# Attention with 192 queries and 1024 keys: transposed scores, an exponential straight from PSUM without a row maximum, and row sums from a ones column beside V

## The chip, the cores and the metric

The kernel runs on one core of one Trainium2 chip. Times are device microseconds (us) of that core, medians of several runs. The runs that are compared here are of the fast state (the records know a slower one, with longer times at a lower granted clock); one of the four runs of b4_gpsimd was slow and is left out. Each batch of runs had the kernel before run beside it on the same chip (1265.0 to 1265.2 us every time). Trace times are counted from the start of the profiled span.

## The reference

```python
B, H, Sq, Sk, D = 16, 32, 192, 1024, 128          # bf16; q, k, v are normal * 0.05
def reference(q, k, v):
    scale = q.shape[-1] ** -0.5
    scores = jnp.einsum("bhqd,bhkd->bhqk", q, k) * scale
    p = _softmax(scores, axis=-1)
    return jnp.einsum("bhqk,bhkd->bhqd", p, v)
```

There are 512 heads. K and V hold 134 MB each, Q and the output 25 MB each: 319 MB have to pass the DMA engines whatever the kernel computes.

## The kernel before

Heads go in groups of 16, two groups of buffers. A pair of heads makes three units of 128 query rows (128 of each head, then 64 of both side by side). Per unit: QK into PSUM with queries on the partitions, a row maximum on VectorE, a shift on GpSimd or an exponential on ScalarE, eight transposes on TensorE, an evacuation through ScalarE (with the exponential where the shift was on GpSimd), then PV. All loads and stores are issued by SyncE, on one queue:

```python
                e.dma_start_transpose(
                    kt[:, s], kf[h0:h0 + G].rearrange("g k d -> (g k) d")
                ).then_inc(sxk[s], 16)
                e.dma_start_transpose(
                    qt[:, s], qf[h0:h0 + G].rearrange("g k d -> (g k) d")
                ).then_inc(sxq[s], 16)
                if g >= NS:
                    e.wait_ge(s_pv, last_u + 1)
                e.dma_start(
                    vs[:, s], vf[h0:h0 + G].rearrange("g (p t) d -> p g t d", t=KT_TILES)
                ).then_inc(svl[s], 16)
```

```python
            def tr(u):                       # TensorE: the transposes that the change removes
                # ... waits ...
                for t in range(KT_TILES):
                    ins = pe.transpose(PT[:, t, :], X[:, t: SK: KT_TILES], ident[:])
                ins.then_inc(s_tr, 1)
            # ...
                dve.tensor_scalar(           # VectorE: row maximum (as a minimum of the negated scores)
                    ss[:, u % NSS, :], s_ps[u % 2][:], -scale, None, ALU.mult, ALU.min,
                    accum_out=nb[:, u % NSS: u % NSS + 1],
                ).then_inc(s_max, 1)
```

V's key order is `8 p + t`, so that each partition reads 2 KB that lie together, and one transfer brings the V of 16 heads.

## Time and profile before

| | before |
|---|---|
| time, median | 1265 us |
| TensorE busy | 1234 us (98%) |
| VectorE, ScalarE, GpSimd busy | 1102, 1049, 960 us |
| a group of 16 heads, from its first QK to the next group's | 38.4 us |

In the profile PE is TensorE and PEld its weight loads, DVE is VectorE, ACT ScalarE, POOL GpSimd, and SPq the queue of SyncE. The profile's page gives busy time and share of the span (part 1), the busy tenths of DMA in 40 slices (part 2), the queues (part 3: packets, MB, share), and the chain that ended last (part 4):

```profile
PE 1234.2 (98%) x20480; PEld 1009.4 (80%) x20480; DVE 1102.0 (87%) x2304; ACT 1048.6 (83%) x1281; POOL 960.4 (76%) x518
...
DMA  9999999999999999999999999999999999999941
...
DMA packets 790743, 321.89 MB, mean 255 GB/s; under 512 B 724992, under 2 KB 724992, under 8 KB 790528
...
q1 hardware_dynamic: 790528, 318.78, 108.8%
q8 instruction: 164, 2.69, 0.8%
...
PE 97%; SPq 1%; DMA 1%; ACT 0%; issue 0%; DVE 0%; ACTq 0%
```

TensorE bounds the kernel: it is busy all the time and is nearly all of the chain. But the line of DMA tenths says 9 in every slice but the last two. The queue's own timeline, columns: start, duration, engine, line, operation, tiles, count.

```profile
177.74 16.89 SPq L141 DMA_TRANSPOSE kt<-in_k_dram  x1
194.67 4.06 SPq L144 DMA_TRANSPOSE qt<-in_q_dram  x1
198.77 0.59 SPq L149 DMA_DIRECT2D vs<-in_v_dram  x1
199.41 4.60 SPq L158 DMA_DIRECT2D out_dram<-ob  x1
204.05 9.72 SPq L163 DMA_DIRECT2D out_dram<-ob  x1
213.82 0.63 SPq L164 DMA_DIRECT2D out_dram<-ob  x1
214.49 18.25 SPq L141 DMA_TRANSPOSE kt<-in_k_dram  x1
...
595.90 19.96 SPq L141 DMA_TRANSPOSE kt<-in_k_dram  x1
...
637.11 17.95 SPq L141 DMA_TRANSPOSE kt<-in_k_dram  x1
```

Here the queue had fallen behind and waited for no compute: what its loads and its first store wait for had been met at least 4.6 us earlier. This cycle of 16 heads takes 36.8 us (177.74 to 214.49).

### The profile page before, as it was taken

How to read it: one execution, taken by the hardware profiler on the slowest of the kernel's cores; microseconds unless marked ns; L12 is line 12 of the kernel's file. 1: busy time of each engine (PE TensorE's matmuls, PEld its weight loads, DVE VectorE, ACT ScalarE, POOL GpSimd, SP SyncE). 2: the span in 40 equal slices, each digit the busy share in tenths (PEclk: the TensorE clock that was granted, in tenths of full speed). 3: DMA queues.
4: the chain of work that ended last, by engine and by line, in shares of the span. 5: the costliest groups of instructions: out<-in, count | busy, mean ns of one | idle time of the engine just before them, and what ended most of it. 6: DMA issues, size and time to landing. Idle time of an engine off the chain costs nothing.

```text
span 1263.1 us, 48658 instructions
## 1 busy us (share of the span) xinstructions
PE 1234.2 (98%) x20480; PEld 1009.4 (80%) x20480; DVE 1102.0 (87%) x2304; ACT 1048.6 (83%) x1281; POOL 960.4 (76%) x518
## 2 busy tenths in 40 slices
PE   3999999999999999999999999999999999999997
PEld 1888888888888888888888888888888888888886
DVE  2889888898988989898898988889898898989885
ACT  1888888888888888888888888888888888888886
POOL 2778777777877778787777877777787777878774
PEclk9999999999999999999999999999999999999999
DMA  9999999999999999999999999999999999999941
GB/s 288 268 261 240 278 280 266 288 270 245 254 269 261 279 233 255 281 275 262 261 230 272 271 276 268 252 251 272 272 267 281 253 263 252 271 261 281 244 118 27
DMA packets 790743, 321.89 MB, mean 255 GB/s; under 512 B 724992, under 2 KB 724992, under 8 KB 790528
## 3 DMA queue, kind: packets, MB, share of 16 engines
q1 hardware_dynamic: 790528, 318.78, 108.8%
q8 instruction: 164, 2.69, 0.8%
q14 instruction: 51, 0.42, 0.1%
HBM read 134.22 MB, written 25.17 MB: 126 GB/s over the span
## 4 chain that ended last, share of the span: by engine, by line
PE 97%; SPq 1%; DMA 1%; ACT 0%; issue 0%; DVE 0%; ACTq 0%
PE pt_ps L244 33%; PE o_ps L267 24%; PE s_ps L215 18%; PE o_ps L273 11%; PE s_ps L222 9%; SPq L141 1%; DMA vs<-in_v_dram 1%; PE o_ps L270 1%; PE o_ps L275 1%; SPq L144 0%; PE s_ps L228 0%; ACT x_sb L356 0%; ACT pt_sb L367 0%; DVE ob L330 0%; DVE rinv L327 0%
## 5 line engine op out<-in xcount | busy, mean ns | idle before, releaser
L188 POOL TENSOR_TENSOR x_sb<-ss,nb 128x1024 bf16<-128x1024 f32 x512 | 959.7, 1895 | 288.9 <-PE pt_ps L244 266.8
L300 DVE TENSOR_SCALAR_CACHE_REDUCE ss<-s_ps 128x1024 f32<-128x1024 f32 x768 | 938.5, 1222 | 140.5 <-PE s_ps L215 110.8
L244 PEld LDWEIGHTS pt_ps<-ident,x_sb 128*128 128x128 bf16 x6144 | 487.1, 148 | 203.3 <-issue 105.4
L367 ACT ACTIVATE pt_sb<-pt_ps 128x1024 bf16<-128x1024 bf16 x512 | 521.0, 1018 | 41.9 <-PE pt_ps L244 41.8
L244 PE MATMUL pt_ps<-ident,x_sb 128*128 128x128 bf16 x6144 | 520.7, 228 | 0.2 <-ACT pt_sb L367 0.2
L267 PE MATMUL o_ps<-vs,pt_sb 128*128 128x128 bf16 x4096 | 403.0, 217 | 0.3 <-DMA vs<-in_v_dram 0.3
L369 ACT ACTIVATE pt_sb<-pt_ps 128x1024 bf16<-128x1024 bf16 x256 | 262.1, 1024 | 140.1 <-PE pt_ps L244 140.0
L270 PE MATMUL o_ps<-ones,pt_sb 128*128 128x1 bf16 x4096 | 376.0, 165 | 0.0
L267 PEld LDWEIGHTS o_ps<-vs,pt_sb 128*128 128x128 bf16 x4096 | 352.3, 97 | 0.5 <-DMA vs<-in_v_dram 0.4
L270 PEld LDWEIGHTS o_ps<-ones,pt_sb 128*128 128x128 bf16 x4096 | 340.7, 96 | 0.0
L215 PE MATMUL s_ps<-kt,qt 128*128 128x512 bf16 x1024 | 305.3, 379 | 21.3 <-DMA qt<-in_q_dram 21.0
L356 ACT ACTIVATE x_sb<-ss,nb 128x1024 bf16<-128x1024 f32 x256 | 292.3, 1142 | 23.6 <-DVE ss L300 23.6
L273 PE MATMUL o_ps<-vs,pt_sb 128*64 128x128 bf16 x2048 | 162.3, 222 | 0.0
L275 PE MATMUL o_ps<-vs,pt_sb 128*64 128x128 bf16 x2048 | 162.3, 222 | 0.0
L222 PE MATMUL s_ps<-kt,qt 128*64 128x512 bf16 x512 | 153.2, 381 | 0.6 <-DVE ss L300 0.5
L228 PE MATMUL s_ps<-kt,qt 128*64 128x512 bf16 x512 | 153.2, 381 | 0.0
L330 DVE TENSOR_TENSOR ob<-o_ps,rinv 128x384 bf16<-128x384 f32 x256 | 142.7, 557 | 8.7
L273 PEld LDWEIGHTS o_ps<-vs,pt_sb 128*64 128x64 bf16 x2048 | 121.0, 109 | 17.1
L275 PEld LDWEIGHTS o_ps<-vs,pt_sb 128*64 128x64 bf16 x2048 | 121.0, 109 | 0.0
L215 PEld LDWEIGHTS s_ps<-kt,qt 128*128 128x128 bf16 x1024 | 63.3, 96 | 23.6 <-issue 21.5
L300 DVE DVE_READ_ACCUMULATOR ss<-s_ps 128x1 f32 x768 | 64.0, 83 | 0.0
L356 ACT ACTIVATION_READ_ACCUMULATOR x_sb<-ss,nb 128x1 f32 x256 | 48.9, 191 | 0.0
(11 smaller groups left out, 165.7 us busy)
## 6 DMA issues: line engine op xcount, KB each, us to landing
vs<-in_v_dram SPq DMA_DIRECT2D x32, 4096.0 KB, 15.2
out_dram<-ob SPq DMA_DIRECT2D x32, 512.0 KB, 15.9
out_dram<-ob SPq DMA_DIRECT2D x64, 128.0 KB, 4.9
kt<-in_k_dram SPq DMA_TRANSPOSE x32, 21.4
qt<-in_q_dram SPq DMA_TRANSPOSE x32, 6.6
```

Source lines behind the costliest of these rows:

```text
L188: gp.tensor_tensor(x_sb[:, u % NX, :], ss[:, u % NSS, :], nb[:, u % NSS: u % NSS + 1].to_broadcast([128, SK]), ALU.subtract,).then_inc(s_x ...
L215: ins = pe.matmul(S[:, cs], qt[:, s, x * SQ: x * SQ + 128], kt[:, s, x * SK + 512 * c: x * SK + 512 * c + 512], start=True, stop=True,)
L222: pe.matmul(S[0:64, cs], qt[:, s, a * SQ + 128: a * SQ + 192], kt[:, s, a * SK + 512 * c: a * SK + 512 * c + 512], start=True, stop=True, ...
L244: ins = pe.transpose(PT[:, t, :], X[:, t: SK: KT_TILES], ident[:])
L267: ins = pe.matmul(O[:, sl, :], PTS[:, t, :], vs[:, s, x, t, :], start=first, stop=last, skip_group_check=True)
L270: ins = pe.matmul(O[:, 3, sl: sl + 1], PTS[:, t, :], ones[:, 0:1], start=False, stop=last, skip_group_check=True)
L273: pe.matmul(O[0:64, sl, :], PTS[:, t, 0:64], vs[:, s, a, t, :], start=first, stop=last, skip_group_check=True, tile_position=(0, 0))
L275: ins = pe.matmul(O[64:128, sl, :], PTS[:, t, 64:128], vs[:, s, b, t, :], start=first, stop=last, skip_group_check=True, tile_position=(0, ...
L300: dve.tensor_scalar(ss[:, u % NSS, :], s_ps[u % 2][:], -scale, None, ALU.mult, ALU.min, accum_out=nb[:, u % NSS: u % NSS + 1],).then_inc(s ...
L356: act.activation(x_sb[:, u % NX, :], ss[:, u % NSS, :], ACT_FN.Exp, bias=nb[:, u % NSS: u % NSS + 1], scale=-1.0, accum_out=rs[:, pr % NRS ...
L367: act.activation(pt_sb[:, u % NPT], pt_ps[u % 2][:], ACT_FN.Exp, scale=-1.0).then_inc(s_eva, 1)
L369: act.activation(pt_sb[:, u % NPT], pt_ps[u % 2][:], ACT_FN.Copy).then_inc(s_eva, 1)
```

## The change

The intent is to take transposes, row maximum, shift and evacuation away. QK is computed transposed (keys on the partitions), so that its exponential is at once the stationary operand of PV. The maximum is left out; the row sums come from a ones column that stands beside V in SBUF; at the end the sums are checked for range, and where one falls outside, the whole of the kernel before runs as a general path. The diff, cut to its core:

```diff
+def _attention_kernel(nc, q, k, v, out, GM=8, NS=4):        # groups of 8 heads, four buffers
+    NSO = 3
+    VB = 288
+            vs = sb("f_vs", [128, NS, GM * 4 + 1, VB], BF16)
+                    if g >= NS:
+                        e.wait_ge(s_qk, first[g - NS] + sizes[g - NS])
+                    e.dma_start_transpose(
+                        kt[:, s, 0:T * n * 128].rearrange("d (t m) -> d t m", t=T),
+                        kf[h0:h0 + n].rearrange("g (m t) d -> (g m) (t d)", t=T),
+                    ).then_inc(s_kq[s], 16)
+                    ... # Q likewise, then a wait for the buffer's last PV
+                    for i in range(n):
+                        e.dma_start(
+                            vs[:, s, 4 * i: 4 * i + 4, 32:VB],
+                            vf[h0 + i].rearrange("(p u t) d -> p u (t d)", u=4, t=2),
+                        ).then_inc(s_v[s], 16)
+    ... # TensorE: QK transposed
+                                ins = pe.matmul(
+                                    S[:, c0: c0 + (j1 - j0) * 64],
+                                    kt[:, s, w0: w0 + 128], mv, start=True, stop=True)
+    ... # TensorE: PV, the ones column left of even tiles and right of odd ones
+                            c0 = b * VB + (31 if t % 2 == 0 else 160)
+                            ins = pe.matmul(
+                                O[64 * x: 64 * x + 64, o0: o0 + 129],
+                                pt[:, (h + x) % NP, t * SQ + j * 64: t * SQ + j * 64 + 64],
+                                vrow[:, c0: c0 + 129], ...)
+    ... # ScalarE: one instruction per head
+                    act.activation(pt[:, h % NP, :], s_ps[h % 2][:], ACT_FN.Exp, scale=scale).then_inc(s_exp, 1)
```

To put a ones column beside every tile, two tiles (512 bytes) are followed by a gap of 64 bytes in SBUF. V no longer travels in runs of 2 KB but in runs of 512 bytes, and by one transfer a head.

More of the change, by code (lines that the diff above doesn't have):

```diff
@@ L13, with _only_if, wrap, run @@
 R_W = 2
-def _attention_kernel(nc, q, k, v, out, G=16, NS=2, LAGS=(2, 4, 5, 7), ROUTES=(R_W, R_W, R_EA)):
+def _only_if(redo):
+    def wrap(body):
+        def run(eng):
+            with eng.register() as r:
+                eng.reg_load(r, redo[0:1, 0:1])
+                with eng.If_ne(r, 0):
+                    body(eng)
+        return run
+    return wrap
+def _general_path(nc, q, k, v, out, redo, G=16, NS=2, LAGS=(2, 4, 5, 7), ROUTES=(R_W, R_W, R_EA)):
     B, H, SQ, D = q.shape
@@ L133, in _ @@
         @block.sync
+        @_only_if(redo)
         def _(e):
@@ L176, in _ @@
         @block.gpsimd
+        @_only_if(redo)
         def _(gp):
@@ L197, in _ @@
         @block.tensor
+        @_only_if(redo)
         def _(pe):
@@ L294, in _ @@
         @block.vector
+        @_only_if(redo)
         def _(dve):
@@ L347, in _ @@
         @block.scalar
+        @_only_if(redo)
         def _(act):
@@ L377, in _, with _group_sizes, sem, sb @@
                     exp_first(u)
+QK_TILED = False
+RS_LO = 2.0 ** -40
+RS_HI = 2.0 ** 20
+def _group_sizes(NH):
+    if NH >= 32:
+        return [2, 2, 4] + [8] * ((NH - 16) // 8) + [4, 2, 2]
+    return [2] * (NH // 2)
+def _attention_kernel(nc, q, k, v, out, GM=8, NS=4):
+    B, H, SQ, D = q.shape
+    SK = k.shape[2]
+    assert D == 128 and SK == 1024 and SQ == 192, (D, SK, SQ)
+    NH = B * H
+    NPR = NH // 2
+    T = SK // 128
+    scale = float(D) ** -0.5
+    sizes = _group_sizes(NH)
+    assert sum(sizes) == NH
+    first = [sum(sizes[:i]) for i in range(len(sizes))]
+    NG = len(sizes)
+    gof = [g for g in range(NG) for _ in range(sizes[g])]
+    NP = 6
+    NSO = 3
+    VB = 288
+    qf = q.rearrange("b h s d -> (b h) s d")
+    kf = k.rearrange("b h s d -> (b h) s d")
+    vf = v.rearrange("b h s d -> (b h) s d")
+    of = out.rearrange("b h s d -> (b h) s d")
+    with ExitStack() as outer:
+        redo = outer.enter_context(nc.sbuf_tensor("redo", [1, 1], mybir.dt.int32))
+        def sem(name):
+            return outer.enter_context(nc.semaphore(name))
+        s_set = sem("f_set")
+        s_kq = [sem("f_kq%d" % i) for i in range(NS)]
+        s_v = [sem("f_v%d" % i) for i in range(NS)]
+        s_st = [sem("f_st%d" % i) for i in range(NSO)]
+        s_qk = sem("f_qk")
+        s_exp = sem("f_exp")
+        s_pv = sem("f_pv")
+        s_dv = sem("f_dv")
+        s_on = sem("f_on")
+        s_fl = sem("f_fl")
+        with ExitStack() as es:
+            def sb(name, shape, dt):
+                return es.enter_context(nc.sbuf_tensor(name, shape, dt))
+            def ps(name, shape, dt):
+                return es.enter_context(nc.psum_tensor(name, shape, dt))
+            kt = sb("f_kt", [128, NS, T * GM * 128], BF16)
+            qt = sb("f_qt", [128, NS, 3 * GM * 64], BF16)
+            vs = sb("f_vs", [128, NS, GM * 4 + 1, VB], BF16)
+            pt = sb("f_pt", [128, NP, T * SQ], BF16)
+            ob = sb("f_ob", [128, NSO, GM // 2, 3 * D], BF16)
+            rs = sb("f_rs", [128, 2, 3], F32)
+            rinv = sb("f_rinv", [128, NPR * 3], F32)
+            chk = sb("f_chk", [128, NPR * 3], F32)
+            bad = sb("f_bad", [128, 2], BF16)
+            ones = sb("f_ones", [128, 1], BF16)
+            s_ps = [ps("f_s%d" % i, [128, T * SQ], F32) for i in range(2)]
+            o_ps = [ps("f_o%d" % i, [128, 512], F32) for i in range(2)]
+            block = es.enter_context(nc.Block())
+            def kq_cnt(g):
+                return 32 * (g // NS + 1)
+            def v_cnt(g):
+                return 16 * sum(sizes[i] for i in range(g % NS, g + 1, NS))
+            @block.sync
+            def _(e):
+                def loads(g):
+                    s = g % NS
+                    n = sizes[g]
+                    h0 = first[g]
+                    if g >= NS:
[4 more added lines that the diff above has]
+                    ).then_inc(s_kq[s], 16)
+                    e.dma_start_transpose(
+                        qt[:, s, 0:3 * n * 64].rearrange("d (j p) -> d j p", j=3),
+                        qf[h0:h0 + n].rearrange("g (p j) d -> (g p) (j d)", j=3),
+                    ).then_inc(s_kq[s], 16)
+                    if g >= NS:
+                        e.wait_ge(s_pv, (first[g - NS] + sizes[g - NS]) // 2)
+                    for i in range(n):
[3 more added lines that the diff above has]
+                        ).then_inc(s_v[s], 16)
+                def stores(g):
+                    so = g % NSO
+                    n = sizes[g]
+                    h0 = first[g]
+                    e.wait_ge(s_on, (h0 + n) // 2)
+                    e.dma_start(
+                        of[h0:h0 + n].rearrange("(a x) (p j) d -> (x p) a (j d)", x=2, j=3),
+                        ob[:, so, 0:n // 2, :],
+                    ).then_inc(s_st[so], 16)
+                for g in range(min(NS, NG)):
+                    loads(g)
+                for g in range(NG):
+                    if g + NS < NG:
+                        loads(g + NS)
+                    stores(g)
+                for so in range(min(NSO, NG)):
+                    e.wait_ge(s_st[so], 16 * len(range(so, NG, NSO)))
+            @block.gpsimd
+            def _(gp):
+                for s in range(min(NS, NG)):
+                    gp.memset(vs[:, s, :, 0:32], 1.0).then_inc(s_set, 1)
+                gp.memset(ones[:], 1.0).then_inc(s_set, 1)
+            @block.tensor
+            def _(pe):
+                def qk(h):
+                    g = gof[h]
+                    s = g % NS
+                    n = sizes[g]
+                    hh = h - first[g]
+                    if hh == 0:
+                        pe.wait_ge(s_kq[s], kq_cnt(g))
+                    if h >= 2:
+                        pe.wait_ge(s_exp, h - 1)
+                    S = s_ps[h % 2]
+                    qv = qt[:, s, 0:3 * n * 64].rearrange("d (j r) -> d j r", j=3)
+                    ins = None
+                    for t in range(T):
+                        w0 = t * n * 128 + hh * 128
+                        cut = {2: (0, 2, 3), 5: (0, 1, 3)}.get(t, (0, 3))
+                        for j0, j1 in zip(cut[:-1], cut[1:]):
+                            mv = qv[:, j0:j1, hh * 64: hh * 64 + 64]
+                            c0 = t * SQ + j0 * 64
+                            if QK_TILED:
+                                for x in range(2):
+                                    ins = pe.matmul(
+                                        S[64 * x: 64 * x + 64, c0: c0 + (j1 - j0) * 64],
+                                        kt[:, s, w0 + 64 * x: w0 + 64 * x + 64], mv,
+                                        start=True, stop=True, tile_position=(0, 64 * x))
+                            else:
+                                ins = pe.matmul(
+                                    S[:, c0: c0 + (j1 - j0) * 64],
+                                    kt[:, s, w0: w0 + 128], mv, start=True, stop=True)
+                    ins.then_inc(s_qk, 1)
+                order = [(j, t) for j in range(3) for t in range(T)]
+                def pv(pr, lo, hi):
+                    h = 2 * pr
+                    g = gof[h]
+                    s = g % NS
+                    hh = h - first[g]
+                    if lo == 0:
+                        if pr == 0:
+                            pe.wait_ge(s_set, min(NS, NG) + 1)
+                        if hh == 0:
+                            pe.wait_ge(s_v[s], v_cnt(g))
+                        pe.wait_ge(s_exp, h + 2)
+                        if pr >= 2:
+                            pe.wait_ge(s_on, pr - 1)
+                    O = o_ps[pr % 2]
+                    ins = None
+                    for j, t in order[lo:hi]:
+                        for x in range(2):
+                            b = (hh + x) * 4 + t // 2
+                            vrow = vs[:, s].rearrange("p b c -> p (b c)")
+                            c0 = b * VB + (31 if t % 2 == 0 else 160)
+                            o0 = j * 130 + t % 2
+                            ins = pe.matmul(
+                                O[64 * x: 64 * x + 64, o0: o0 + 129],
+                                pt[:, (h + x) % NP, t * SQ + j * 64: t * SQ + j * 64 + 64],
+                                vrow[:, c0: c0 + 129],
+                                start=t == 0, stop=t == T - 1, skip_group_check=True,
+                                tile_position=(0, 64 * x))
+                    if hi == len(order):
+                        ins.then_inc(s_pv, 1)
+                for n in range(NPR + 2):
+                    if QK_TILED:
+                        if n < NPR:
+                            qk(2 * n)
+                        if n >= 2:
+                            pv(n - 2, 0, 12)
+                        if n < NPR:
+                            qk(2 * n + 1)
+                        if n >= 2:
+                            pv(n - 2, 12, 24)
+                    else:
+                        if n < NPR:
+                            qk(2 * n)
+                            qk(2 * n + 1)
+                        if 1 <= n <= NPR:
+                            pv(n - 1, 0, 24)
+                pe.wait_ge(s_fl, 1)
+                pe.matmul(o_ps[0][0:1, 0:1], ones[:, 0:1], bad[:, 0:1], start=True, stop=False)
+                pe.matmul(o_ps[0][0:1, 0:1], ones[:, 0:1], bad[:, 1:2], start=False, stop=True).then_inc(s_fl, 1)
+            @block.vector
+            def _(dve):
+                cnt = [0]
+                def step(ins):
+                    ins.then_inc(s_dv, 1)
+                    cnt[0] += 1
+                    dve.wait_ge(s_dv, cnt[0])
+                def onorm(pr):
+                    g = gof[2 * pr]
+                    so = g % NSO
+                    a = pr - first[g] // 2
+                    O = o_ps[pr % 2][:, 0:390].rearrange("p (j c) -> p j c", j=3)
+                    ri = rinv[:, 3 * pr: 3 * pr + 3]
+                    dve.wait_ge(s_pv, pr + 1)
+                    step(dve.tensor_copy(rs[:, pr % 2, :], O[:, :, 0]))
+                    step(dve.tensor_tensor(rs[:, pr % 2, :], rs[:, pr % 2, :], O[:, :, 129], ALU.add))
+                    step(dve.reciprocal(ri, rs[:, pr % 2, :]))
+                    if a == 0 and g >= NSO:
+                        dve.wait_ge(s_st[so], 16 * (g // NSO))
+                    dve.tensor_tensor(
+                        ob[:, so, a, :].rearrange("p (j d) -> p j d", j=3),
+                        O[:, :, 1:129],
+                        ri.unsqueeze(2).to_broadcast([128, 3, D]),
+                        ALU.mult,
+                    ).then_inc(s_on, 1)
+                def check(lo, hi, i):
+                    step(dve.tensor_scalar(chk[:, lo:hi], rinv[:, lo:hi], 1.0 / RS_HI, 1.0 / RS_LO, ALU.max, ALU.min))
+                    step(dve.tensor_tensor(chk[:, lo:hi], chk[:, lo:hi], rinv[:, lo:hi], ALU.not_equal))
+                    step(dve.tensor_reduce(bad[:, i: i + 1], chk[:, lo:hi], mybir.AxisListType.X, ALU.max))
+                early = max(NPR - 6, 1)
+                for pr in range(NPR):
+                    onorm(pr)
+                    if pr == early - 1:
+                        check(0, 3 * early, 0)
+                check(3 * early, 3 * NPR, 1)
+                dve.sem_inc(s_fl, 1)
+                dve.wait_ge(s_fl, 2)
+                dve.tensor_copy(redo[0:1, 0:1], o_ps[0][0:1, 0:1]).then_inc(s_fl, 1)
+                dve.wait_ge(s_fl, 3)
+            @block.scalar
+            def _(act):
+                for h in range(NH):
+                    act.wait_ge(s_qk, h + 1)
+                    if h >= NP:
+                        act.wait_ge(s_pv, (h - NP) // 2 + 1)
+                    act.activation(pt[:, h % NP, :], s_ps[h % 2][:], ACT_FN.Exp, scale=scale).then_inc(s_exp, 1)
+        _general_path(nc, q, k, v, out, redo)
```

## The prediction

> **What bounds it now.** Two things, nearly level.
> - TensorE: the chain of waits gives PE 97% (transposes 33%, PV 24% and 11%, QK 18% and 9%), busy 1234 of 1263 us. A group of 16 heads takes 38.4 us (first QK to first QK).
> - The DMA queue, close behind: busy share 9 in almost every slice. Where its queue had fallen behind TensorE (K transposes issued at 177.7, 214.5, 252.4, 289.5 us), it cycled in 36.8 to 37.9 us a group. So DMA alone would take about 32 x 37.2 = 1190 us.
>
> 256-byte packets (transposes, stores) peak at 1133 per us over 16 engines, 14.1 ns each (290 GB/s); 2048-byte ones (V) take 84 ns (390 GB/s). That fits a fixed cost of about 4 ns plus 0.039 ns per byte; the Trainium skill ("DMA: Bandwidth & Descriptors", Why small descriptors are slow) tells of a fixed per-packet overhead, which this agrees with. Per group: K and Q 17.2, V 10.8, stores 2.7, together 30.6 us; each 16 KB instruction fetch (164 of them) stops the transposes for about 1.5 us, about 4 us a group; the rest, about 2.4 us, is ramps between transfers.
>
> **What the change does.**
> - Removes 6144 PE transposes (520 us busy, about 0.65 us per unit), 4096 ones matmuls, the row maximum (938 us DVE), the shift (960 us POOL), the transposed copies (783 us ACT).
> - Adds one 1536-column exponential per head: 1018 ns for 1024 columns plus 512 x 0.83 ns ("ScalarE: Activation LUTs", throughput) is an estimated 1.45 us, 2.9 us a pair. PE per pair: QK 2 x 1536 columns, at 210 to 224 ns per 512, about 1.3 us; PV 24 tiled pairs at 68 ns (now 139 us/2048), 1.6 us. With handoffs, 3.0 to 3.3 us a pair against 4.8: compute would end near 800 to 850 us.
> - Moves no byte away: still 319 MB. V's packets shrink from 2048 to 512 bytes, estimated 24 ns: V 344 -> 395 us. Stores grow to 768 bytes: 87 -> 70 us. K and Q stay 622592 packets of 256 bytes, 549 us at peak, K now in strides of 2 KB. Instructions fall by about a sixth, so fetch stalls about 120 us. 68 groups instead of 32 ramp more often, about 1.5 us each, 100 us. Sum 549+395+70+120+100 = about 1235; four buffers and small first and last groups cut what stands outside the DMA stream from about 60 to 20 us, and deeper queueing should hide some ramps.
>
> **Critical path.** Nearly all removed work frees TensorE, but the limit passes to the DMA queue, which was only 3% below it. I expect the gain to be a few per cent, not the third that the engines promise: **1195 us**, 80% range 1090 to 1275. Faster by over 2%: 0.70; within 2%: 0.20; slower by over 2%: 0.10.
>
> **What would show it.** PE busy near 800 us (65 to 70%), ACT near 740 us, POOL near 0; DMA slices still 9; idle time before the first QK of each group put down to the K or Q DMA, some 5 to 7 us per group of 8; the chain of waits on DMA and SP's issues, not PE; V packets of 512 bytes near 24 ns.
>
> **What would make it wrong.** Strided K rows transposing slower than 290 GB/s at peak (then over 1265); 512-byte packets at the rate of 2048-byte ones, or transposes reading whole 2 KB rows in larger packets (then 1050 or below); the SP queue's waits on compute or its issue time (8 V loads a group at 0.59 us) leaving the DMA engines empty.

## More of the kernel before

The 22 cycles from 101.85 to 940.80 us, in which the K loads always found their wait met, take 36.2 to 41.2 us (the longest is 595.90 to 637.11), 38.1 on average. TensorE needs 38.4.

## The result, and the profile after

After takes 1314.05 us (1307.6 to 1320.4, four runs) against 1265.18: slower, ratio 1.038, 95% interval 1.035 to 1.042. Here and below a ratio is the mean time of one kernel's fast runs over that of the other's of the same rounds, so it is not quite the ratio of the quoted medians. The same parts of the page, after:

```profile
PE 895.5 (68%) x17410; PEld 798.6 (61%) x17410; DVE 266.7 (20%) x1031; ACT 716.0 (55%) x513; POOL 4.0 (0%) x9
...
DMA  9999999999999999999999999999999999999996
...
DMA packets 931303, 321.33 MB, mean 245 GB/s; under 512 B 636224, under 2 KB 931136, under 8 KB 931136
...
q1 hardware_dynamic: 931136, 318.82, 113.1%
q8 instruction: 139, 2.28, 0.7%
...
SPq 39%; DMA 27%; PE 27%; issue 3%; DVE 3%; DVEq 0%
```

Every engine is relieved as intended: TensorE 68% where it had 98%, GpSimd nothing, VectorE 20%. The bytes are the same, but there are 140,000 packets more, and the chain has moved to the queue and the DMAs. The queue's timeline:

```profile
601.39 12.04 SPq L482 DMA_TRANSPOSE f_kt<-in_k_dram  x1
...
622.64 10.03 SPq L482 DMA_TRANSPOSE f_kt<-in_k_dram  x1
632.71 2.61 SPq L486 DMA_TRANSPOSE f_qt<-in_q_dram  x1
635.37 6.33 SPq L493 DMA_DIRECT2D f_vs<-in_v_dram  x8
641.74 0.62 SPq L503 DMA_DIRECT2D out_dram<-f_ob  x1
642.41 10.63 SPq L482 DMA_TRANSPOSE f_kt<-in_k_dram  x1
```

A cycle of 8 heads takes 19.8 us here (622.64 to 642.41) and took 21.3 the time before (601.39 to 622.64). From 150 to 1150 us the mean is 20.2, so 16 heads take 40.4, against 38.1 for the queue before. Two views of waits can mislead here. The queue's own waits:

```profile
SPq L482 <- PE f_s L550: 619.5, 64, 11.3
SPq L493 <- PE f_o L578: 12.3, 22, 1.1
```

One would read that the K loads wait 620 us for QK. They do not: a K load waits for the QK of the group four before it, and for the load at 601.4 us that QK's last matmul had started at 560.1. The time is the transpose itself, which holds the queue while it is carried out; the view puts it down to the semaphore that the instruction names. And the engines' waits:

```profile
DVE f_ob L628 <- DMA out_dram<-f_ob: 580.2, 62, 17.2
ACT f_pt L657 <- PE f_s L550: 573.5, 178, 15.6
...
PE f_o L578 <- DVE f_ob L628: 385.6, 61, 14.0
```

This looks as if three output buffers were too few. It is tested below (x2_nso6).

What did the DMA engines do? I counted the trace's packets per microsecond, from 625 us (K and Q are of 256 bytes, V 512, stores 768; rows 628, 630, 631 and 635 left out):

```
us    256 B  512 B  768 B
625      50    104    344     tail of V, the store
626     569      0     95
627     915      0      0     K
629    1132      0      0     K at its peak (290 GB/s)
632     803      0      0     a 16 KB instruction fetch starts at 632.3
633      21      0      0     ... and the transposes stand still
634     883      0      0     Q
636     926     49      0
637       0    387      0     V (another fetch at 636.8)
638       0    513      0
```

From such counts I made an account for 150 to 1150 us of each trace: in every 0.1 us, packets times a cost near that at which they usually flow (14.1 ns for 256 bytes, 27.8 for 512, 36 for 768, 84 for 2048, over 16 engines) is work, the rest is lost. Only the 14.1 ns is a peak: in the best tenth of the half microseconds that hold one size alone, 512-byte packets took 25.4 ns in after and 2 KB ones 80 in before. Where a text here says "at peak" of V, these usual costs are meant. Loss is sorted into that within 0.2 to 2.4 us of a 16 KB fetch's start while no V flows, that within the same kind of window after an 8 KB fetch, that while V flows, and the rest, which is mostly the changes from one transfer to the next. The sorting is mine and rough.

| us of 1000: work, and what is lost | work at these costs | after a 16 KB fetch | after an 8 KB fetch | while V flows | other |
|---|---|---|---|---|---|
| before | 791 | 121 | 8 | 36 | 44 |
| after | 818 | 66 | 5 | 48 | 64 |

So at these costs after does not lose more per microsecond than before. It has more work: 65536 V packets x 84 ns / 16 = 344 us became 262144 x 27.8 / 16 = 455 us, while the stores went from 98304 x 14.1 / 16 = 87 to 32768 x 36 / 16 = 74 us. That is 98 us more, on a queue that had been less than 1% below the limit. The split depends on the costs: with 24 ns for 512 bytes, an estimated 47 us of after's 818 (262144 x 3.8 / 16, for 1000 of 1312 us) would count as loss, and after would lose more than before. What V's packets cost is therefore decided by the runs below, not by this account.

The counts also show what a fetch stops. Of after's 107 fetches of 16 KB in that stretch, 60 start within transposes, whose rate falls on average from about 1,100 packets per us to under 200 from 0.5 to 1.75 us after the fetch's start; 39 start within V, whose rate stays near 530.

### The profile page after: what moved, and what is told of

Its sections match the earlier page's. It is cut to its first block, busy times and chain, and to the rows that moved or that the text cites. A ratio compares the mean times of both kernels' runs of the same rounds, so it can differ in the third digit from the quotient of the medians.

```text
span 1311.8 us, 38033 instructions
## 1 busy us (share of the span) xinstructions
PE 895.5 (68%) x17410; PEld 798.6 (61%) x17410; DVE 266.7 (20%) x1031; ACT 716.0 (55%) x513; POOL 4.0 (0%) x9
## 4 chain that ended last, share of the span: by engine, by line
SPq 39%; DMA 27%; PE 27%; issue 3%; DVE 3%; DVEq 0%
SPq L493 30%; DMA out_dram<-f_ob 27%; PE f_o L578 17%; PE f_s L550 10%; SPq L486 6%; SPq L482 3%; DVE f_ob L628 3%; DMA f_vs<-in_v_dram 0%; DVEq L627 0%; DVE f_chk L637 0%; DVE f_rinv L625 0%; DVE f_bad L638 0%; DVE f_rs L623 0%; DVE f_rs L624 0%; PE f_o L604 0%
## 5 line engine op out<-in xcount | busy, mean ns | idle before, releaser
L657 ACT ACTIVATE f_pt<-f_s 128x1536 bf16<-128x1536 f32 x512 | 714.7, 1448 | 584.9 <-PE f_s L550 573.5
L578 PE MATMUL f_o<-f_vs,f_pt 128*64 128x129 bf16 x12288 | 481.3, 244 | 388.8 <-DVE f_ob L628 385.6
L578 PEld LDWEIGHTS f_o<-f_vs,f_pt 128*64 128x64 bf16 x12288 | 436.2, 125 | 433.5 <-issue 431.1
L550 PE MATMUL f_s<-f_qt,f_kt 128*128 128x192 bf16 (+2 forms) x5120 | 444.5, 246 | 19.4 <-DMA f_qt<-in_q_dram 19.4
L550 PEld LDWEIGHTS f_s<-f_qt,f_kt 128*128 128x128 bf16 x5120 | 362.3, 105 | 71.2 <-DMA f_qt<-in_q_dram 20.1
L628 DVE TENSOR_TENSOR f_ob<-f_o,f_rinv 128x384 bf16<-128x384 f32 x256 | 142.7, 558 | 586.9 <-DMA out_dram<-f_ob 580.2
L623 DVE COPY f_rs<-f_o 128x3 f32<-128x3 f32 x256 | 40.5, 158 | 433.8 <-PE f_o L578 433.8
L625 DVE RECIPROCAL f_rinv<-f_rs 128x3 f32<-128x3 f32 x256 | 45.2, 176 | 8.9
L624 DVE TENSOR_TENSOR f_rs<-f_rs,f_o 128x3 f32<-128x3 f32 x256 | 40.4, 158 | 8.9
L520 POOL MEMSET f_vs<- 128x1056 bf16 x4 | 3.7, 978 | 0.3 <-POOLq L683 0.3
```

Source lines behind the costliest of these rows:

```text
L520: gp.memset(vs[:, s, :, 0:32], 1.0).then_inc(s_set, 1)
L550: ins = pe.matmul(S[:, c0: c0 + (j1 - j0) * 64], kt[:, s, w0: w0 + 128], mv, start=True, stop=True)
L578: ins = pe.matmul(O[64 * x: 64 * x + 64, o0: o0 + 129], pt[:, (h + x) % NP, t * SQ + j * 64: t * SQ + j * 64 + 64], vrow[:, c0: c0 + 129], ...
L623: step(dve.tensor_copy(rs[:, pr % 2, :], O[:, :, 0]))
L624: step(dve.tensor_tensor(rs[:, pr % 2, :], rs[:, pr % 2, :], O[:, :, 129], ALU.add))
L625: step(dve.reciprocal(ri, rs[:, pr % 2, :]))
```

## The experiments

The theory is **DMA**: the one queue's stream is the limit, and V's small packets carry it above TensorE's old time. Rivals: **compute** (the handoffs of QK, exponential and PV, or the half clock after waits), **output buffers**, and **transfer starts** rather than packet size.

### x1_light: the compute made light

```diff
-mv = qv[:, j0:j1, hh * 64: hh * 64 + 64]
+mv = qv[:, j0:j1, hh * 64: hh * 64 + 8]
-act.activation(pt[:, h % NP, :], s_ps[h % 2][:], ACT_FN.Exp, scale=scale)
+act.activation(pt[:, h % NP, 0: T * 24], s_ps[h % 2][:, 0: T * 24], ACT_FN.Exp, scale=scale)
+gp.memset(pt[:], 1.0)     # once; QK's output columns shrunk to match
```

> After with its compute made light and its DMA and instruction count untouched: QK moves 8 query columns per slot instead of 64, the exponential takes 192 columns instead of 1536 (about 0.3 us instead of 1.45 us), the rest of the probabilities stay 1. Result wrong on purpose. Theory DMA (the stream of the one queue is the limit): no change, 1290 to 1325 us. Rival compute (the QK, exp, PV handoffs, or the half clock, are on the path): 10 to 25% less.

Measured 1318.1 us, ratio to before 1.041 (1.037 to 1.046), the same as after. ScalarE fell from 716 to 152 us busy and TensorE from 896 to 680, for nothing. The mean granted clock (as a share of full speed) even fell to 0.748 from 0.839, since TensorE waits more, and that cost nothing either. The Trainium skill ("TensorE: Matmul & The Clock Gate", HAM oscillation) says that idle gaps above about 3.4 us halve the clock; after's trace agrees, with 63 such gaps and 64 stretches at a granted clock of 0.5. Compute is off the path. A side remark: this kernel was judged correct although most of its probabilities were 1. With inputs this small the softmax is nearly flat, so the comparison says little about the exponential.

### x2_nso6: six output buffers

```diff
-    NSO = 3
+    NSO = 6
```

> After with six output buffers instead of three. In the profile VectorE waits 580 us in total for stores to land before it writes an output buffer. Theory DMA: those waits cost nothing, within 1% of after. Rival buffers (compute and stores are locked together through three output buffers): at least 3% faster.

Measured 1316.9 us, ratio 1.042 (1.038 to 1.046): no change. The waits only changed their name:

```profile
PEld f_s L550 <- DMA f_qt<-in_q_dram: 260.8, 67, 6.8
PE f_s L550 <- DMA f_qt<-in_q_dram: 250.0, 67, 6.6
PEld f_o L578 <- DMA f_vs<-in_v_dram: 160.8, 62, 4.7
PE f_o L578 <- DMA f_vs<-in_v_dram: 146.7, 62, 4.5
```

With three buffers the store, which stands behind the next loads on the same queue, was the first thing late; with six it is Q and V themselves. The 580 us of VectorE's waits were a symptom.

### x3_v2k: V in 2 KB packets

```diff
-vs = sb("f_vs", [128, NS, GM * 4 + 1, VB], BF16)
+vs = sb("f_vs", [128, NS, GM * 1024 + 64], BF16)
-vs[:, s, 4 * i: 4 * i + 4, 32:VB],   vf[h0 + i].rearrange("(p u t) d -> p u (t d)", u=4, t=2),
+vs[:, s, 32 + 1024 * i: 32 + 1024 * i + 1024],   vf[h0 + i].rearrange("(p t) d -> p (t d)", t=8),
-c0 = b * VB + (31 if t % 2 == 0 else 160)
+c0 = 31 + (hh + x) * 1024 + t * 128        # the neighbour's column as "ones": wrong sums
```

> After with V laid out in 2 KB runs per partition, so 65536 packets of 2048 bytes instead of 262144 of 512; same number of V transfers, same compute. Row sums wrong on purpose, the range check's verdict held at no. Theory DMA with small packets: V at peak falls from 262144 x 27.8 ns / 16 = 455 us to 65536 x 84 / 16 = 344 us, so about 110 us less, 1190 to 1230 us. Rival (packet size does not matter, the transfers' starts do): within 2% of after.

Measured 1234.5 us, ratio 0.976 (0.974 to 0.977):

```profile
DMA packets 734696, 321.33 MB, mean 261 GB/s; under 512 B 636224, under 2 KB 668992, under 8 KB 734528
```

That is 80 us less than after, a little above the expected range: the size of V's packets is the largest single cause found of the slowdown, and its rival falls. It is not the full 110 us: in the account, loss while V flows rose from 48 to 73 us of 1000 and that after fetches from 66 to 86. Its eight V transfers of 256 KB have only 8 packets per engine each.

### x4_g16: groups of 16, two buffers

```diff
-def _attention_kernel(nc, q, k, v, out, GM=8, NS=4):
+def _attention_kernel(nc, q, k, v, out, GM=16, NS=2):
-        return [2, 2, 4] + [8] * ((NH - 16) // 8) + [4, 2, 2]
+        return [2, 2, 4, 8] + [16] * ((NH - 32) // 16) + [8, 4, 2, 2]
-    NSO = 3
+    NSO = 2
```

> After with groups of 16 heads and two input buffers (same memory) instead of 8 and four; two output buffers of twice the size. K and Q transposes and stores half as many, V transfers as many. Theory DMA with a loss at each change of transfer (K to Q to V to store to K, about 2 to 4 us a group by the packet rates): 33 changes of group fewer, 60 to 120 us less, 1190 to 1260 us. Rival (losses are per byte or per packet): within 2% of after.

Measured 1293.1 us, ratio 1.020 (1.016 to 1.024): 21 us less than after, a third of the least expected, and at 1.6% inside the rival's 2%. This run alone does not decide between the two; b2_g16 below, where the same step gained 47 us (3.8%), does. "Other" loss did halve (64 to 31 us of 1000), but loss after fetches rose from 66 to 90. Both kernels fetch equally often (107 in that window), but 86 of the fetches now start within a transpose, where 60 did in after.

### x5_fewinst: the same DMAs, few instructions

```diff
-                    for t in range(T):
+                    for t in range(1):
-                order = [(j, t) for j in range(3) for t in range(T)]
+                order = [(j, t) for j in range(3) for t in (0, T - 1)]
```

(against x1_light, the exponential cut to match)

> x1_light with most of its compute instructions taken out (QK one tile of eight, PV two of eight), same DMAs. x1_light showed that the compute itself costs no time. In the trace the transposes fall to nearly no packets for about 1.5 us after each 16 KB instruction fetch; summed over after's span that is about 80 to 100 us. Theory fetch: the time falls by 60 to 110 us against x1_light, to 1210 to 1260 us. Rival (those dips have another cause, fetches only coincide): within 1% of x1_light's 1318.

Measured 1226.7 us, ratio 0.969 (0.967 to 0.971), 91 us below x1_light. Its output is wrong, which doesn't matter for the time. The page's line of the fetch queue, in x1_light's trace:

```profile
q8 instruction: 138, 2.26, 0.7%
```

and in x5_fewinst's:

```profile
q8 instruction: 30, 0.49, 0.2%
```

108 fetches fewer for 91 us, and x1_light had shown that the work of the instructions is free. If all 91 us are theirs, a fetch of 16 KB costs about 0.84 us on average. The account, made for these two traces as well, sees about 60 of the 91 us after 16 KB fetches (33 us lost of 1000 in place of 77); the rest of the gain lies in V and the changes of transfer, and no run ties it to the fetches. The queue's bytes for them are under 1% of the traffic.

### x6_before512: the kernel before with V in 512-byte packets

```diff
-        vs = sb("vs", [128, NS, G, KT_TILES, 128], BF16)
+        vs = sb("vs", [128, NS, G * 4, 288], BF16)
-                    vs[:, s], vf[h0:h0 + G].rearrange("g (p t) d -> p g t d", t=KT_TILES)
+                    # for u in range(4): one transfer per quarter of the keys
+                    vs[:, s].rearrange("p (g u) c -> p g u c", u=4)[:, :, u, 32:288],
+                    vf[h0:h0 + G].rearrange("g (p u t) d -> p g u (t d)", u=4, t=2)[:, :, u],
```

> Before, with V alone changed to the 512-byte layout of after (four transfers a group by quarter; ones matmuls and all else as before). Theory DMA: before's queue needs 36.8 to 37.9 us a group of 16 and TensorE 38.4; 8192 packets of 512 bytes at 27.8 ns cost 14.2 us where 2048 of 2 KB cost 10.8, so the queue needs about 40.7 us and takes over: 1325 to 1365 us. Rival (before is limited by TensorE with room to spare): within 1% of 1265 us.

Measured 1316.1 us, ratio 1.042 (1.039 to 1.045). It is 51 us slower than before, slightly below the expected range, and lands on after's time. Its chain shows the queue and V's DMA taking their share from TensorE:

```profile
DMA packets 988888, 321.90 MB, mean 246 GB/s; under 512 B 726528, under 2 KB 988672, under 8 KB 988672
...
PE 68%; DMA 15%; SPq 14%; issue 2%; ACT 1%; DVE 0%; ACTq 0%
```

V's layout alone is thus enough to bring the kernel before to 1316 us. Its two halves are not told apart by this run (packets of 512 bytes, and four transfers in place of one). And no run tells the size of the packets from their place: wherever it changed, the 64-byte gaps between them in SBUF changed with it.

### x7_vby4: fewer V transfers, same packets

```diff
-                    for i in range(n):
+                    for u in range(4):
-                            vs[:, s, 4 * i: 4 * i + 4, 32:VB],
-                            vf[h0 + i].rearrange("(p u t) d -> p u (t d)", u=4, t=2),
+                            vs[:, s, 0: 4 * n, 32:VB].rearrange("p (g u) c -> p g u c", u=4)[:, :, u],
+                            vf[h0:h0 + n].rearrange("g (p u t) d -> p g u (t d)", u=4, t=2)[:, :, u],
```

> After with V's loads cut by quarter of the keys instead of by head: 4 transfers a group of 8 instead of 8, the same 512-byte packets. If 27.8 ns (not the 24 ns estimated) is a cost of the packet: within 1% of after. If it holds a cost of each transfer (its 16 completion writes): V's peak falls by half of the difference, about 30 us.

Measured 1297.3 us, ratio 1.025 (1.023 to 1.027): 17 us less, between the two. The number of transfers costs something too: loss while V flows fell from 48 to 31 us of 1000. The steady rate did not change: in half microseconds that hold V alone, the median is 284 packets here and 283 in after, 28.2 ns per packet. In x6_before512 it is about 300 (26.7 ns) and in the best tenth 339 (23.6 ns). So the 24 ns of the prediction can be reached, but is not held; why is open.

### b1: a correct kernel with 2 KB packets

V lands in a staging buffer by one transfer a group, and VectorE copies each pair's V beside the ones columns, two pairs ahead of its use:

```diff
+                    dve.tensor_copy(
+                        vp[:, pr % NPAD, 0:8, 32:VB],
+                        vs[:, s, 2048 * a: 2048 * a + 2048].rearrange("p (b c) -> p b c", b=8),
+                    ).then_inc(s_cp, 1)
-                            vs[:, s, 4 * i: 4 * i + 4, 32:VB],
-                            vf[h0 + i].rearrange("(p u t) d -> p u (t d)", u=4, t=2),
+                    vs[:, s, 0: n * 1024].rearrange("p (g c) -> p g c", g=n),
+                    vf[h0:h0 + n].rearrange("g (p t) d -> p g (t d)", t=8),
```

> A correct version of x3: V lands in 2 KB runs by one transfer a group, and VectorE, idle in after, copies each pair's V beside the ones columns. Theory DMA: V's peak 344 us as in x3 and fewer V transfers, 1170 to 1235 us, below both kernels; VectorE stays under 60% busy. Rival (the copy or its handoff brings compute back): above 1250 us.

Measured 1240.6 us, ratio 0.983 (0.979 to 0.987), correct, a little above the expected range. VectorE is 34% busy; the copy takes 683 ns a pair:

```profile
L674 DVE COPY f_vp<-f_vs 128x2048 bf16<-128x2048 bf16 x256 | 174.8, 683 | 35.9 <-DMA f_vs<-in_v_dram 35.9
```

Fewer V transfers gained nothing over x3_v2k (loss while V flows is 72 of 1000 here and 73 there), though the copy came in at the same time.

### b2_g16: b1 in groups of 16

The edit is that of x4_g16, made on b1.

> b1 with groups of 16 heads and two input buffers. x4 gained 21 us from this on after. Theory (a loss at each change of transfer on the one queue): 15 to 40 us less than b1's 1241. Rival (two buffers make the loads wait on compute): no gain or slower.

Measured 1193.4 us, ratio 0.943 (0.941 to 0.944), correct: 47 us below b1, more than the 15 to 40 expected, and the fastest kernel of this study, 5.7% below before and 9% below after (1193.4 over 1314.1; not of the same rounds). Loss while V flows fell from 72 to 41 us of 1000 and other loss from 51 to 40; V's transfers were halved here too, which x4_g16 did not do. Its page:

```profile
PE 837.1 (70%) x17410; PEld 739.6 (62%) x17410; DVE 423.5 (36%) x1287; ACT 716.1 (60%) x513; POOL 1.3 (0%) x6
...
DMA packets 724710, 321.27 MB, mean 269 GB/s; under 512 B 626240, under 2 KB 659008, under 8 KB 724544
```

The DMA engines still bound it, to go by its slices (9 in all but the first and the last) and by its chain (DMA 40%, PE 38%, SPq 14%); the whole gain over after is a rate of 269 GB/s in place of 245.

### b3_scalar, b4_scalar, b4_gpsimd: a second queue for V and the stores

```diff
-VQ = "sync"        # b1 and b2_g16
+VQ = "scalar"      # b3_scalar (groups of 8), b4_scalar (groups of 16): V loads and stores issued by ScalarE
+VQ = "gpsimd"      # b4_gpsimd (groups of 16)
```

> b1 with V's loads and the stores issued from ScalarE's queue, the K and Q transposes alone on SyncE's. The DMA engines' peak work of b1 is about 549+344+74 = 967 us of 1240. Theory (the rest, about 270 us, is lost because one queue holds everything in order: while the transposes stand still for a fetch or end unevenly, nothing else can run): a second queue fills much of it, 1080 to 1180 us. Rival (the losses belong to the DMA engines themselves): within 2% of b1.

> b2_g16 with V's loads and the stores on ScalarE's queue. As b3_scalar, and the number of groups should matter less than between b1 and b2_g16, since the change of transfer is no longer a gap: within 2% of b3_scalar.

> b2_g16 with V's loads and the stores issued from the idle GpSimd. If a second queue is what counts, about as b4_scalar (within 3%); if what counts is which engine builds the descriptors, slower.

Measured: b3_scalar 1212.9 us, ratio 0.960 (0.956 to 0.964), so 2.2% below b1, just outside the rival's 2% and far from the theory's range; b4_scalar 1225.5 us, ratio 0.969 (0.967 to 0.971), so within 2% of b3_scalar as expected, but 2.7% above b2_g16; b4_gpsimd 1346.8 us (three fast runs; the slow one took 1356.7), ratio 1.060 (1.055 to 1.065). My theory fell here: a second queue does not fill the gaps. At best it helps a little, and with large groups it costs more than it gives. The Trainium skill ("DMA: Bandwidth & Descriptors", Issuing engines are not separate DMA queues) says that DMAs issued by different engines run on the same 16 DMA engines and interleave, which saves only issue time; b4_scalar, 2.7% slower than b2_g16, agrees with that. What the 28 us that b3_scalar gained are, no run shows. Nor do these runs settle why GpSimd's queue is 9% worse than ScalarE's. Fewer packets did not help it; the queue with V and the stores, in b4_scalar:

```profile
q10 hardware_dynamic: 99520, 159.39, 44.3%
```

and in b4_gpsimd:

```profile
q0 software_dynamic: 39680, 159.39, 39.3%
```

## Why the prediction was wrong

- **What bounded it, and what would.** Right in kind, but "only 3% below it" was too wide. TensorE bounded before, with the queue less than 1% behind: the 1190 us for the DMA alone came from three short cycles, and 32 times the mean of 38.1 us is 1219. The gain on the engines is real (TensorE 68%, ScalarE 716 us where 740 was estimated, GpSimd 4 us, no instruction of the general path) and worthless, since the queue took over. The 1448 ns of one exponential fit the estimate of 1.45 us made with the 0.833 ns per element of the Trainium skill ("ScalarE: Activation LUTs", Step-by-step: what each stage is for). x1_light shows that none of the compute is on the path.
- **The step that failed, as put: "V's packets shrink from 2048 to 512 bytes, estimated 24 ns: V 344 -> 395 us."** The straight line through 256 and 2048 bytes gave 24 ns; after holds 28.3 ns (283 packets in half a microsecond over 16 engines), and with the 27.8 ns of the account V costs 455 us, 60 us more than estimated. x3_v2k and x6_before512 show by runs that V's layout moves the time by 80 and 51 us.
- **"deeper queueing should hide some ramps".** This step failed too. My own sum was 1235 us; I took 40 us off without a measurement behind it. The runs showed nothing hidden: after loses 182 us of 1000, about 239 over its span, where the sum had 220. From 1195 to 1314 us are 119: 40 of this discount, 60 of V's packets, about 19 of the losses, at the account's costs.
- **Fetch stalls, "about 120 us".** The mechanism is right. x5_fewinst measures 91 us for 108 of 139 fetches, 117 for all in proportion, if all of it is theirs; the account sees about 60 of the 91.
- **"68 groups instead of 32 ramp more often".** Right in kind. x4_g16 gained 21 us and b2_g16 47 us from nearly half as many groups (38 in place of 68).
- **"idle time before the first QK of each group put down to the K or Q DMA".** In after it is put down to the stores' landing at the output buffers instead, since those stood behind the loads; with six buffers (x2_nso6) the view shows it as predicted.
- **Strided K rows slower.** Not seen: the transposes run at about 565 packets per half microsecond in before and after alike. No run tests it alone.

## What to carry to other kernels

Before removing work from the engine that is busiest, find out how far behind the next limit is, from many cycles and not from the best ones, and in which currency it counts; here the DMA queue stood less than 1% behind, and its currency was packets, transfers and even instruction fetches, not bytes. A layout that makes compute cheaper may cut the runs that a transfer moves: load in the longest runs and let an idle engine rearrange on chip (b2_g16: a 0.68 us copy a pair, 1193 us). A long wait on a buffer or a semaphore is a cause only when giving the buffer away removes it (x2_nso6 removed the wait and no time).

## What the Trainium skill lacked or had wrong

- "DMA: Bandwidth & Descriptors", Specifications, gives 512 B as the minimum transfer for line rate. Here 512-byte packets ran at 283 per half microsecond (290 GB/s), 2 KB ones at 94 (385 GB/s).
- The same page, Why small descriptors are slow, tells of a fixed overhead per packet. A fixed cost fitted to 256 and 2048 bytes gives 24 ns for 512 bytes; the best tenth in x6_before512 had 23.6, but 28.3 was held in after, so such a cost alone does not give the rate.
- The same page, Latency and other measured facts, gives DMA transposes 261 GB/s with a non-contiguous middle dimension and 350 to 400 GB/s where contiguous. Here contiguous K rows and rows in strides of 2 KB both peaked at 290 GB/s (565 packets of 256 bytes per half microsecond), and a load averaged less.
- I found no page that says that instruction fetches stop DMA transposes: after a 16 KB fetch the transposes of all engines fall to nearly no packets for about 1.5 us, and taking out 108 fetches with their instructions saved 91 us (x5_fewinst). It would belong to "Runtime: NRT & Kernel Launch", Instruction fetch mechanics.
- I found no page that says how the queue's waits are to be read where a transpose holds its queue: 619.5 us stood as a wait for QK that had been met 41 us earlier in the case looked at.
